# Low bits by PoolE, sign by VectorE, a bias table one block later, and extra matmuls between the first chunks

## The chip, the cores and the metric

One core of a Trainium2 chip runs the kernel. The time is that of one execution on the device in microseconds (us); lower is better. PE is TensorE, DVE is VectorE, ACT is ScalarE, POOL is PoolE (GpSimd), and SP is the engine that issues most DMA transfers. [...]

## What is computed

Three layers follow each other on 4 x 768 = 3072 tokens of width 256. The first is a scan in chunks (8 heads of width 32, state 16), the second a dense two-matrix layer, the third a gated mixture of 8 experts, of which each token takes one.

```python
M = CB * L                                  # within a chunk, L = exp of sums of log a, lower triangle
y = M @ x + (C @ state) * exp(cum)          # plus what the state carries in
state = exp(sum) * state + sum(B x decay)   # from chunk to chunk
h = x @ w_in;  g = max(0.01 * h, h);  x = g @ w_out
logits = x @ w_gate + modality_bias[modality_id];  e = argmax(logits)
out = gate * (max(x @ w1[e], 0) @ w2[e])
```

The weights w_in and w_out come as 64-bit floats. The matrices of the second layer are multiplied as pairs of a rounded high part and a rest, three products for each.

## The kernel before

The scan works in 24 chunks of 128 tokens. The first four (block 0) run ahead of everything else; the other chunks are woven into the matmuls of the dense layer, which runs in six blocks of 512 tokens with 16 steps each (mm1 gives h, mm2 gives y). The expert layer follows at the end.

For each of the first four chunks the loop at L916 calls, in this order: attn_cd (scales C, tile cd), attn_tr (transposes of C and B into ps; from them cbd on VectorE and btt on ScalarE), attn_exp_pe (broadcast matmuls bc, exponentials e on ScalarE, masks of e by affine_select on PoolE), attn_tr2, attn_cb twice (product cb; VectorE multiplies e by it), and p3 (products psy, state st). For chunk 0 the broadcast is built from laT and tri; for chunks 1 to 3 from cumb, a tile with three bfloat16 parts of the running sums. cumb is made by decay: p_212 and p__232 are transposed sums, cr and cumb their residuals on VectorE, cend their last columns, pd a small product of cend.

Between the chunks stand pieces of work from the list early: the loads and splits of w_in and w_out. A piece is 128 x 512 numbers; there are 16. to_f32 (L529) turns the 64-bit words into float32: ScalarE makes hb from the upper half word, PoolE writes lb as whole 32-bit words, VectorE overwrites one 16-bit half of each lb, and then VectorE joins hb and lb. split casts the result to the high part (wih, woh) on ScalarE and subtracts it on PoolE or VectorE into the rest (wil, wol). Loads go to three buffers raw, and each waits until the pieces in its buffer are done.

bias_table makes a table of 3072 x 8 biases from modality_id with six VectorE instructions; block 0's route, in block 1, is the first to read it. The table Q holds the step at which such work is put into the blocks ('bt': 4 is step 4 of block 0).

Nine matmuls of zeros (wps<-zer, bfloat16, 128 x 512) stand at the start. The order on each engine is made by a scheduler from the order in the code; functions named in Q['pin'] keep program order on the engines given there ('t' is PE). Each engine runs its queue in order.

Of the kernel before, what the change touches and what calls it, by code (L numbers as in the profile page):

```python
# [14 lines left out]
ALU = mybir.AluOpType  # L15
# [5 lines left out]
LOW, LOW0 = 0.9 * 2.0 ** -13, 0.2995  # L21
# [3 lines left out]
Q = {'sg': (0, 1),  # L25
 'i00': 0,
 'i01': 1,
 'lo1': -1,
 'o00': 0,
 'o01': 4,  # L30
 'i10': 3,
 'i11': 3,
 'xe': 2,
# [12 lines left out]
 'r0': 6,  # L46
 'r1': 6,
 'xt': 14,
 'bt': 4,
 'cv': 2,  # L50
 'cvn': 3,
 'tr': 4,
# [31 lines left out]
         'L_rows_out': 's',  # L84
         'L_m2_xT': 'v',
         'S_attn_cb': 't',
         'S_split_win': 'g',
         'S_split_wout': 'v',
         'S_load_wout': 'vsg',
# [9 lines left out]
def kernel(  # L99
# [20 lines left out]
    NE, _, F2 = w1.shape  # L120
    P = 128
# [48 lines left out]
    v, s, g, t_ = Pinned(nc.vector, "v"), Pinned(nc.scalar, "s"), Pinned(nc.gpsimd, "g"), Pinned(nc.tensor, "t")  # L170

    def run(fn, args, late=""):
        for e in (v, s, g, t_):
            e.on = e.key in Q["pin"].get(late + fn.__name__, "")
        fn(*args)
        for e in (v, s, g, t_):
            e.on = False
# [351 lines left out]
    def to_f32(raw, q):  # L529

        w = raw.bitcast(I32).rearrange("p (f w) -> p f w", w=2)
        hb = ap_.tile([P, 512], F32, tag="hb", name="hb")
        lb = ap_.tile([P, 512], I32, tag="lb", name="lb")
        s.activation(out=hb, in_=w[:, :, 1].bitcast(F32), func=AF.Copy, scale=2.0 ** -112)
        w4 = raw.bitcast(U16).rearrange("p (f w) -> p f w", w=4)
        l2 = lb.bitcast(U16).rearrange("p (f w) -> p f w", w=2)
        g.tensor_scalar(out=lb, in0=w4[:, :, 3], scalar1=32768.0, scalar2=-(2.0 ** 31), op0=ALU.is_ge, op1=ALU.mult)
        v.tensor_scalar(out=l2[:, :, 0], in0=w4[:, :, 1], scalar1=LOW, scalar2=LOW0, op0=ALU.mult, op1=ALU.add)
        hi = hb.bitcast(I32)
        v.scalar_tensor_tensor(out=hi, in0=hi, scalar=3, in1=lb, op0=ALU.logical_shift_left, op1=ALU.bitwise_or)  # L540
        return hb
# [13 lines left out]
    def split_win(k, kk):  # L555
        r = raws["i", k]
        os = slice(k * 512, (k + 1) * 512)
        f = to_f32(r[:, kk, :], kk) if W64 else r[:, kk, :]
        split(f, wih[:, kk, os], wil[:, kk, os], g if kk in Q["sg"] else v)
# [6 lines left out]
    def split_wout(k, q):  # L566
        r = raws["o", k]
        os = slice(k * 4 + 2 * q, k * 4 + 2 * q + 2)
        f = r[:, 2 * q:2 * q + 2, :].rearrange("p a d -> p (a d)")
        f = to_f32(f, q) if W64 else f  # L570
        split(
            f, woh[:, os, :].rearrange("p a d -> p (a d)"), wol[:, os, :].rearrange("p a d -> p (a d)"), g if q in Q["sg"] else v
        )
# [314 lines left out]
    wt = zer  # L888
    v.memset(wt, 0.0)
    wps = psh.tile([P, 512], F32, tag="h", name="wps")  # L890
    for _ in range(Q["warm"]):
        t_.matmul(wps, lhsT=wt[:, 0:P], rhs=wt, start=True, stop=True)
    nb = len(blocks)
    NC0 = blocks[0][1] // P
    new_xt(0)
# [19 lines left out]
            run(fn, args, "S_")  # L915
    for c in range(NC0):  # L916
        for fn, *args in (
            (attn_cd, c), (attn_tr, c), (attn_exp_pe, c), (attn_tr2, c), (attn_cb, c, 0), (attn_cb, c, 1), (p3, c),
        ):
            run(fn, args, "S_")  # L920
        for fn, args, w in early:
            if w == c:
                run(fn, args, "S_")
# [143 lines left out]
```

## Time and profile before

| | us |
|---|---|
| median of 3 runs | 552.48 |
| lowest, highest | 550.47, 555.38 |
| profiled execution | 552.29 |
| its span | 550.6 |

| engine | busy us | share of the span |
|---|---|---|
| PE | 519.3 | 94% |
| DVE | 365.0 | 66% |
| ACT | 334.0 | 61% |
| POOL | 199.2 | 36% |

The busy shares are means over stages with different limits. The time of the stages and the waits are read from the windows and the time lines below. A busy PE at half clock does half the work.

### The profile page before, as it was taken

The page shows a single profiled execution, that of the slowest core. Times are in us where ns is not written, and L with a number is a line of the kernel's source. Part 1 is how long each engine was busy: PE and PEld are TensorE (multiplying, and loading weights), DVE is VectorE, ACT ScalarE, POOL GpSimd, SP SyncE. Part 2 cuts the span into 40 slices and gives each one's busy share as a digit, 9 for nine tenths or more (in the row PEclk, how much of TensorE's full clock was granted, in tenths as well). Part 3 has the DMA queues.
Part 4 walks back from the last instruction along what each step waited for, and adds up shares of the span by engine and source line. Part 5 has one row for each costly group of instructions (what it writes and reads, how often), then busy time and mean ns, then how long its engine had stood idle before and what let it go on. Part 6 is the DMA issues. An engine that isn't in the chain of part 4 may idle for free.

```text
span 550.6 us, 9529 instructions
## 1 busy us (share of the span) xinstructions
PE 519.3 (94%) x3411; PEld 422.3 (77%) x3411; DVE 365.0 (66%) x714; ACT 334.0 (61%) x699; POOL 199.2 (36%) x167
## 2 busy tenths in 40 slices
PE   6998978999999999999999999999989999999990
PEld 3434654678787878778877787688879999999990
DVE  5658998977667777775667866475577564555630
ACT  5447667675676676765766665354537665666630
POOL 5648798300301120113010301540063466556331
PEclk9559999999999999999999999999999999999996
DMA  8898753212744239322620476345059667777300
GB/s 195 138 226 160 206 143 57 54 34 34 17 116 81 59 43 107 63 59 11 130 60 0 13 139 198 98 31 86 1 187 168 222 210 239 219 236 240 109 23 21
DMA packets 128312, 61.02 MB, mean 111 GB/s; under 512 B 84545, under 2 KB 120514, under 8 KB 128258
## 3 DMA queue, kind: packets, MB, share of 16 engines
q1 hardware_dynamic: 125186, 53.94, 48.2%
q0 software_dynamic: 3072, 6.41, 3.6%
q8 instruction: 29, 0.48, 0.4%
q14 instruction: 25, 0.20, 0.2%
HBM read 53.73 MB, written 6.60 MB: 110 GB/s over the span
## 4 chain that ended last, share of the span: by engine, by line
PE 78%; DVE 8%; issue 5%; ACT 3%; DMA 2%; SPq 1%; POOL 1%; POOLq 0%; DVEq 0%; ACTq 0%
PE y L163 21%; PE h L163 21%; PE hp L163 11%; PE o L163 10%; PE psy L163 5%; PE cb L163 3%; DVE hb L163 1%; DVE gg L163 1%; DMA ct<-in_C_dram 1%; DMA raw<-in_moe_w_in_dram 1%; DVE gl L163 1%; DVE lb L163 1%; PE yr L163 1%; PE pc L163 1%; PE pb L163 1%
## 5 line engine op out<-in xcount | busy, mean ns | idle before, releaser
L163 ACT CAST gh<-gg 128x512 fp32r<-128x512 f32 x96 | 59.6, 621 | 75.6 <-DVE gg L163 74.3
L163 DVE TENSOR_TENSOR gl<-gg,gh 128x512 fp32r<-128x512 f32 x96 | 74.0, 771 | 40.6 <-ACT gh L163 40.0
L163 PE MATMUL h<-xh,wih 128*128 128x512 f32 x192 | 77.7, 408 | 3.9 <-DVE gg L163 3.9
L163 PE MATMUL y<-gl,woh 128*128 128x512 f32 x192 | 76.6, 400 | 3.6 <-DVE gl L163 3.6
L163 DVE TENSOR_TENSOR gg<-sa,h 128x512 f32<-128x512 f32 x96 | 65.3, 681 | 20.5 <-ACT sa L163 20.2
L163 POOL TENSOR_SCALAR_AFFINE_SELECT e<-e 128x1024 f32<-128x1024 f32 (+1 forms) x28 | 28.2, 1012 | 137.9 <-DMA e<-cumd 87.1
L163 PE MATMUL h<-xl,wih 128*128 128x512 f32 x192 | 75.2, 392 | 0.0
L163 PE MATMUL y<-gh,wol 128*128 128x512 f32 x192 | 75.0, 392 | 0.0
L163 PE MATMUL h<-xh,wil 128*128 128x512 f32 x192 | 75.0, 392 | 0.0
L163 PE MATMUL hp<-x2h,w1s 128*128 128x256 f32 x384 | 71.9, 283 | 0.0
L163 PE MATMUL o<-w2s,hh 128*128 128x256 f32 x384 | 69.3, 285 | 0.0
L163 ACT ACTIVATE sa<-h 128x512 f32<-128x512 f32 x96 | 57.2, 596 | 19.0 <-PE h L163 18.4
L163 DVE SCALAR_TENSOR_TENSOR hl<-hp,hh 128x512 fp32r<-128x512 f32 x48 | 33.0, 691 | 52.6 <-ACT hh L163 44.0
L163 PE MATMUL y<-gh,woh 128*128 128x512 f32 x192 | 63.3, 398 | 0.0
L163 PEld LDWEIGHTS hp<-x2h,w1s 128*128 128x128 f32 x384 | 61.1, 192 | 0.6
L163 POOL TENSOR_TENSOR w2s<-r,w2s 128x1024 fp32r<-128x1024 f32 x12 | 34.0, 2838 | 72.7 <-ACT w2s L163 48.7
L163 PEld LDWEIGHTS o<-w2s,hh 128*128 128x128 f32 x384 | 58.4, 191 | 0.4 <-issue 0.4
L163 PE MATMUL hp<-x2l,w1s 128*128 128x256 f32 x192 | 53.3, 283 | 0.0
L163 ACT ACTIVATE hh<-hp 128x512 fp32r<-128x512 f32 x48 | 28.4, 597 | 40.0 <-PE hp L163 35.0
L163 ACT ACTIVATE e<-e,ncum 128x128 f32<-128x128 f32 x160 | 51.5, 395 | 0.0
L163 PE MATMUL o<-w2s,hl 128*128 128x256 f32 x192 | 51.1, 283 | 0.0
L163 POOL DMA_INDIRECT il<-ids,pi x24 | 25.7, 1070 | 66.5 <-DVE pi L163 38.3
(205 smaller groups left out, 1012.3 us busy)
## 6 DMA issues: line engine op xcount, KB each, us to landing
r<-in_moe_w_dram SPq DMA_DIRECT2D x48, 512.0 KB
e<-cumd SPq DMA_DIRECT2D x20, 512.0 KB
raw<-in_moe_w_in_dram SPq DMA_DIRECT2D x4, 1024.0 KB
raw<-in_moe_w_out_dram SPq DMA_DIRECT2D x4, 1024.0 KB
yx<-ysb SPq DMA_DIRECT2D x6, 528.0 KB
xt<-in_x_dram SPq DMA_DIRECT2D x24, 128.0 KB
ct<-in_C_dram SPq DMA_DIRECT2D x24, 64.0 KB
bt<-in_B_dram SPq DMA_DIRECT2D x24, 64.0 KB
```

The lines of the kernel that those rows point to most:

```text
L163: r = f(*args, **kw)
```

## The change

Three edits. In to_f32 PoolE now writes the low bits (multiply and add on half word 1) as whole words of lb, and VectorE the sign (compare and multiply on half word 3) into the upper half of each; before, PoolE wrote the sign and VectorE the low bits into the lower half. bias_table moves from step 4 to step 16, the first step of block 1. And keep puts matmuls of zeros between the parts of each of the first four chunks: 12 or 4, then 2, then 3, in all 44; they are pinned on PE.

```diff
- 'bt': 4,
+ 'bt': 16,
+         'S_keep': 't',
-        g.tensor_scalar(out=lb, in0=w4[:, :, 3], scalar1=32768.0, scalar2=-(2.0 ** 31), op0=ALU.is_ge, op1=ALU.mult)
-        v.tensor_scalar(out=l2[:, :, 0], in0=w4[:, :, 1], scalar1=LOW, scalar2=LOW0, op0=ALU.mult, op1=ALU.add)
+        g.tensor_scalar(out=lb, in0=w4[:, :, 1], scalar1=LOW, scalar2=LOW0, op0=ALU.mult, op1=ALU.add)
+        v.tensor_scalar(out=l2[:, :, 1], in0=w4[:, :, 3], scalar1=32768.0, scalar2=32768.0, op0=ALU.is_ge, op1=ALU.mult)
-    for _ in range(Q["warm"]):
-        t_.matmul(wps, lhsT=wt[:, 0:P], rhs=wt, start=True, stop=True)
+    def keep(n):
+        for _ in range(n):
+            t_.matmul(wps, lhsT=wt[:, 0:P], rhs=wt, start=True, stop=True)
+    keep(Q["warm"])
-            (attn_cd, c), (attn_tr, c), (attn_exp_pe, c), (attn_tr2, c), (attn_cb, c, 0), (attn_cb, c, 1), (p3, c),
+            (attn_cd, c), (attn_tr, c), (attn_exp_pe, c), (keep, 4 if c else 12), (attn_tr2, c), (attn_cb, c, 0), (keep, 2), (attn_cb, c, 1), (keep, 3), (p3, c),
```

The scheduler orders the queues anew. On VectorE, the rows behind the first chunk's cbd stood like this before (the first cbd here is chunk 1's, e is chunk 0's, lb and hb are the first weight piece's):

```order
L163 TENSOR_TENSOR cbd<-ps,gm 128x512
L163 TENSOR_TENSOR cr<-p_212,cumb 64x512
L163 TENSOR_TENSOR bs<-bt,e 128x128
L163 COPY cend<-p__232 32x2
L163 TENSOR_TENSOR cumb<-cr,cumb 32x512
L163 TENSOR_TENSOR cd<-ct,ecum 128x128
L163 COPY cend<-p_212 32x4
L163 TENSOR_TENSOR e<-e,cb 128x512
L163 TENSOR_SCALAR lb<-raw 128x512
```

And now, in the same place (the first lb is that of w_in, the second that of w_out):

```order
L164 TENSOR_TENSOR bs<-bt,e 128x128
L164 TENSOR_SCALAR lb<-raw 128x512
L164 TENSOR_TENSOR cr<-p_212,cumb 64x512
L164 COPY cend<-p__232 32x2
L164 SCALAR_TENSOR_TENSOR hb<-hb,lb 128x512
L164 TENSOR_TENSOR cd<-ct,ecum 128x128
L164 TENSOR_SCALAR lb<-raw 128x512
L164 TENSOR_TENSOR cbd<-ps,gm 128x512
L164 TENSOR_TENSOR cumb<-cr,cumb 32x512
L164 COPY cend<-p_212 32x4
L164 TENSOR_TENSOR e<-e,cb 128x512
```

Two weight pieces moved ahead of cumb, and chunk 1's cbd behind both.

On PoolE, from chunk 2's masks on, the rows stood like this before (128x512 are masks of the first four chunks, two for each; 128x1024 are masks of later chunks, whose e is loaded):

```order
L163 AFFINE_SELECT e<-e 128x512 x2
L163 TENSOR_TENSOR wil<-hb,wih 128x512
L163 AFFINE_SELECT e<-e 128x512 x2
L163 TENSOR_SCALAR lb<-raw 128x512
L163 AFFINE_SELECT e<-e 128x1024 x3
L163 TENSOR_TENSOR wil<-hb,wih 128x512
L163 TENSOR_SCALAR lb<-raw 128x512 x2
L163 AFFINE_SELECT e<-e 128x1024
```

And now:

```order
L164 AFFINE_SELECT e<-e 128x512 x2
L164 AFFINE_SELECT e<-e 128x1024 x3
L164 AFFINE_SELECT e<-e 128x512
L164 AFFINE_SELECT e<-e 128x1024
L164 AFFINE_SELECT e<-e 128x512
L164 TENSOR_SCALAR lb<-raw 128x512
L164 TENSOR_TENSOR wil<-hb,wih 128x512
L164 TENSOR_SCALAR lb<-raw 128x512 x3
```

Chunk 3's two masks moved behind masks of later chunks, and the fourth piece's lb behind all of them.

On PE, from chunk 1's first broadcast matmuls on (each dummy is a LDWEIGHTS and a MATMUL; there are seven at the first "..."), the rows now are:

```order
L164 MATMUL bc<-negm,cumb 128x512
...
L164 MATMUL pd<-cend,bsel 128x6 x4
L164 MATMUL cb<-cbd,btt 128x512
L164 LDWEIGHTS zer
L164 MATMUL wps<-zer 128x512
...
L164 MATMUL ps<-ident,bt 128x128
L164 MATMUL psy<-e,xt 32x128 x8
L164 MATMUL psy<-xt,bs 64x128 x2
```

Chunk 0's second cb and its psy stand behind chunk 1's bc and pd, as before; new are nine dummies between that cb and psy.

## Rows read from the trace of the kernel before

**Rows 1.** Windows: busy us (instructions) of each engine, granted clock, DMA share, GB/s.

```profile
14.00:15.00 1.00, 1.00 (x3) 0.13 (x2) 0.48 (x1) 0.75 (x3) 0.59 (x1) 0.83 0.86 104
15.00:38.00 23.00, 22.79 (x100) 10.73 (x100) 12.86 (x27) 9.87 (x22) 11.67 (x11) 0.50 0.89 176
34.00:38.00 4.00, 4.00 (x16) 2.09 (x17) 2.25 (x5) 2.27 (x5) 0.86 (x2) 0.50 1.10 328
38.00:39.00 1.00, 1.00 (x5) 0.07 (x1) 0.59 (x2) 0.27 (x1) 1.00 (x2) 0.72 1.25 274
39.00:105.00 66.00, 57.67 (x313) 36.62 (x313) 60.14 (x94) 44.15 (x104) 53.78 (x33) 1.00 0.56 128
105.00:500.00 395.00, 390.92 (x2629) 332.41 (x2626) 265.50 (x543) 251.22 (x522) 105.61 (x84) 1.00 0.51 103
```

**Rows 2.** Time line of PE: start us, us, instruction, count, idle before and releaser.

```profile
1.27 3.65 PE L163 MATMUL wps<-zer 128*128 128x512 bf16 x9 [1.27 <-DVE zer L163]
...
12.84 0.33 PE L163 MATMUL ps<-ident,cd 128*128 128x128 f32 x1 [2.25 <-ACT btt L163]
...
14.66 0.61 PE L163 MATMUL bc<-negm,cumb 96*128 96x512 bf16 x1
...
16.49 0.45 PE L163 MATMUL ps<-ident,ct 128*128 128x128 f32 x1
...
17.25 1.87 PE L163 MATMUL pd<-cend,bsel 32*128 32x6 f32 x8
19.05 2.08 PE L163 MATMUL cb<-cbd,btt 64*128 64x512 f32 x4
...
40.76 1.13 PE L163 MATMUL cb<-cbd,btt 64*128 64x512 f32 x4
...
43.12 0.67 PE L163 MATMUL psy<-cdt,st 128*128 128x256 f32 x2 [0.86 <-DVE st L163]
43.72 0.64 PE L163 MATMUL psy<-e,xt 128*32 128x128 f32 x16
44.30 0.44 PE L163 MATMUL psy<-xt,bs 128*64 128x128 f32 x4
```

**Rows 3.** Tiles lb, hb and e: ns min/median/max, first and last start, forms.

```profile
L163 POOL TENSOR_SCALAR lb<-raw x16: 1953/2038/2467, 12.6 to 94.5; 128x512 int32<-128x512 uint16 x16
L163 DVE TENSOR_SCALAR lb<-raw x16: 439/508/1549, 17.5 to 97.2; 128x512 uint16<-128x512 uint16 x16
L163 DVE SCALAR_TENSOR_TENSOR hb<-hb,lb x16: 673/688/1750, 19.8 to 100.1; 128x512 int32<-128x512 int32 x16
L163 POOL TENSOR_TENSOR wil<-hb,wih x8: 1267/1296/1699, 22.6 to 96.9; 128x512 fp32r<-128x512 f32 x8
L163 POOL TENSOR_SCALAR_AFFINE_SELECT e<-e x16: 629/866/1547, 11.0 to 109.3; 128x512 f32<-128x512 f32 x8, 128x1024 f32<-128x1024 f32 x8
```

**Rows 4.** Groups of DVE, 38 to 106 us: count, busy us, mean ns, idle before.

```profile
L163 DVE CAST m<-modi 128x24 f32<-128x24 int32 x1 | 1.1, 1065 | 0.0
L163 DVE TENSOR_SCALAR m<-m 128x24 f32<-128x24 f32 x2 | 0.8, 382 | 0.0
L163 DVE TENSOR_TENSOR btab<-btab,bt 128x192 f32<-128x192 f32 x1 | 0.4, 357 | 0.0
```

**Rows 5.** Time line of DVE: cumb, and the fourth piece's lb.

```profile
13.80 0.68 DVE L163 TENSOR_TENSOR cumb<-cr,cumb 32x512 bf16<-32x512 f32 x1 [0.31 <-ACT cumb L163]
...
41.56 1.18 DVE L163 TENSOR_SCALAR lb<-raw 128x512 uint16<-128x512 uint16 x1
```

**Rows 6.** Time line of POOL: lb of the first, second and seventh piece.

```profile
12.63 1.96 POOL L163 TENSOR_SCALAR lb<-raw 128x512 int32<-128x512 uint16 x1
16.09 2.29 POOL L163 TENSOR_SCALAR lb<-raw 128x512 int32<-128x512 uint16 x1 [1.49 <-DMA raw<-in_moe_w_out_dram]
...
51.66 1.98 POOL L163 TENSOR_SCALAR lb<-raw 128x512 int32<-128x512 uint16 x1 [0.69 <-POOL e L163]
```

**Rows 7.** Chain of waits in block 1: start us, us, what.

```profile
107.20 1.36 PE h L163 x6
```

## The prediction

> **What bounds the kernel now.** I read the windows by stage first, then the time lines of the engines in the first 55 us, then the tiles of the weight split. The windows [rows 1] cut the run by TensorE's granted clock and by who is full. [...] From 39 to 105 us it is full, VectorE is busy 60.1 of 66 us, PoolE 53.8, and PE still has 8.3 us idle. From 105 to 500 us PE is busy 390.9 of 395 us. So after 105 us PE is the bound, and nothing in the diff touches that work: whatever the change does is a shift of the two stages before, and the shift goes one for one into the end.
>
> The first stage is the four chunks of the scan. PE waits 2.25 us before 12.84 us, the clock falls two microseconds later, and it comes back only after 34 to 38 us, where PE is busy 4.00 of 4 us, the last of it with 512-column products; with the narrow matmuls before, PE was busy too and the clock stayed low [rows 1, 2]. The fourth chunk's last matmul ends at 44.30 + 0.44 = 44.74 us [rows 2].
>
> The second stage splits the weights in 16 pieces: for each a PoolE lb (1.95 us at best), a VectorE lb and hb, a cast on ScalarE, and a PoolE subtraction (1.27) [rows 3]. VectorE is nearly full there, in part with waiting: the same lb takes 0.44 at best and 1.55 at worst, hb 0.67 and 1.75 [rows 3].
>
> **The change, part by part.**
>
> *Bias table.* Of its six VectorE instructions at about 74.6 to 78.2 us the cast takes 1.1 us, two scalings together 0.8, an addition 0.4; two products like the addition make it 2.9 us at most, and since neighbouring rows overlap a little I take 2.5 [rows 4]. They leave a stretch where VectorE is full and go to block 1, where VectorE is idle 129.5 of 395 us and the full PE hides them [rows 1]. Without that cover, where one of them delays a gl that PE waits for, the same 2.5 us come back. Gain 2.5 us, bounds 0 and 2.9.
>
> *Low bits and sign swapped.* Each piece keeps one PoolE instruction of 128x512 from 16-bit words into 32-bit words and one VectorE instruction from 16-bit to 16-bit; only the operations in them change places. On VectorE I take the same 0.44 us, bounds 0.44 and the 0.67 of hb. On PoolE no row shows a multiply and add. The lowest row of this size is the affine_select at 0.63 us, the two-input subtraction takes 1.27, the row that it replaces 1.95 to 2.47 [rows 3]. I take 1.95, the row with the same source, destination and number of operations, and keep 0.63 and 2.47 for the range.
>
> *Its place in the queues.* Here I expect the gain of the dummies to go. In the new VectorE order two lb stand ahead of cumb, the residual that chunk 1's broadcast matmuls bc load. Before, cumb ran at 13.80 us and bc began at 14.66 [rows 2, 5]. Now cumb is behind the second lb, whose PoolE instruction waits for the first piece of w_out: that landed at 16.09 us [rows 6]. The loads issued up to it stand in the same order as before, so it lands no earlier. Then PoolE 1.96 to 2.29 us, to 18.05 or 18.4; lb 0.44; cbd of chunk 1 and cumb, 0.6 and 0.6: bc of chunk 1 begins at about 20.0 us, 5.3 us late. Queued behind it on PE are pd, the cb products, nine dummies and the first chunk's psy.
>
> *The dummies.* They are 44 (12 + 3x4 + 4x2 + 4x3). Fourteen stand ahead of that bc and fill time in which PE would wait anyway: no cost. But PE then waits for the late cend (to about 15.9 us) and for cumb (to 20.0), some 5 us of the last 7, more than the gap after which the clock fell before. So I take half clock at 20.0 us. From there at half: bc 1.8 us (14.66 to 16.49), pd 1.8 (17.25 to 19.05), cb 1.0 (two in 2.08), seven dummies at 0.41 (nine in 3.65 at the start, near twice the 0.227 of the full clock) 2.9: 7.5 us, to 27.5 us [rows 2]. This stretch ends as dense with 512 columns as the one after which the clock came back, so I let it come back there. The rest of the four chunks at full clock: 23 dummies at 0.227 (six matmuls in 1.36 us) [rows 7] 5.2; six cb at 0.53 (two in 1.13) 3.2; four psy at 1.0 (43.72 to 44.74) 4.0; three state products at 0.6 (43.12 to 43.72) 1.8; two bc at half of 1.8, 1.8; nine transposes at 0.19 (two in 0.76 at half clock) 1.7 [rows 2]. That is 17.7 us, and the fourth chunk ends at 45.2 us against 44.74: **+0.5 us**.
>
> *PoolE's order.* Chunk 3's masks now stand among four masks of later chunks that wait for their broadcast loads, and the fourth split's lb behind them. Before, that split's VectorE lb ran at 41.56 us [rows 5]. Now PoolE is free for it at about 43.4 (chunk 3's product must be masked 1.8 us ahead of 45.2), lb to 45.4; VectorE's lb, cbd and hb to 47.1, the cast to 47.7, the subtraction to 49.0, three more lb to 55.0 us. Before, the same seventh lb ended at 51.66 + 1.98 = 53.6 [rows 6]. **+1.4 us** on the split chain, bounds 0 (VectorE's idle takes it up) and 3.
>
> *Sum.* +0.5 + 1.4 - 2.5 = -0.6 us. The profiled execution took 552.29 us (span 550.6 and 1.7 around it), 0.2 under the median of 552.48. So about **551.5 us**.
>
> **The rivals.**
>
> R1, multiply and add is cheaper on PoolE. At the 1.27 us of the subtraction, bc of chunk 1 comes 0.7 us earlier and the 13 pieces after 39 us leave PoolE 9 us. Of that the end sees no more than the 8.3 us that PE is idle there [rows 1]; PoolE's wait is one of several, so I put half, 4 us in all: 547.5 us. At 0.63 us, the whole of it: 544. For it speaks that 1.95 us is long beside 1.27 for two inputs; against it, that the kinds of words, the length and the number of operations stay. [...] The affine_select, a compare too, takes 0.63 us here and speaks against a dear compare.
>
> R2, the dummies hold the clock: it does not fall, or is back by 20 us. Then the 7.5 us are 1.6 + 0.9 + 0.9 + 0.5 = 3.9, the fourth chunk ends at 41.6 us, and the lag of the split chain goes: -0.6 - 3.6 - 1.4, about 546.7 us. For it: 14 dummies stand where before PE did little. Against it: the two waits that the late cend and cumb make.
>
> R3, the other side: the dummies run at half clock and so only cost. If it does not rise at 27.5 us, 23 dummies take 9.4 us and the other 12.5 us double: the fourth chunk ends at 61.9 us, +17 us, 568 us. Each microsecond of half clock past 27.5 costs half of one, so it passes 1% if the clock is still low at about 40 us. For it: before, PE was busy for 23 us at half clock without release. Against it: that work was narrow, and four dense microseconds ended it [rows 1].
>
> **How the numbers follow.** About 1%, 5.5 us, is what a measurement of this kernel can tell from no change. Forecast 0.50 (its own range 548 to 556), R1 0.23, R2 0.12, R3 0.15 (half of it late by a few us only, 554 to 558, half above). Faster by over 1% (under 547): nearly half of R1, over half of R2, a little of the forecast, 0.21. Slower (over 558): half of R3 and a little of the forecast, 0.12. Within: 0.67. A range from 545 to 557.5 leaves out a quarter of R1 and of R2 below, half of R3 above, and little of the forecast.
>
> **What would show it.** Right: a granted clock of 0.5 around 20 us and 1.0 before 30; VectorE's second lb just after 18 us and bc of chunk 1 at about 20; chunk 3's psy ending near 45; no bias rows near 75 and VectorE still full there; PoolE's lb at 1.95. Wrong: PoolE's lb at 1.3 or less; a clock that never falls; bc at 15; half clock past 30 us.

## The result and the profile after

| | before | changed |
|---|---|---|
| median, us | 553.51 | 561.65 |
| lowest to highest | 550.47 to 555.38 | 560.95 to 562.76 |
| profiled execution | 552.29 | 561.41 |
| its span | 550.6 | 559.7 |

The ratio is 1.0147, 95% interval 1.0117 to 1.0178: the changed kernel is slower by 1.5%, where 551.5 us (545 to 557.5) was forecast. Three experiments below, e7, e9 and e13, have executions 8 to 12 us apart, some of which the ratios leave out, so nothing is built on one of them alone.

The engines' busy times of the changed kernel: PE 526.6 us, VectorE 361.4, ScalarE 331.9, PoolE 177.9 (199.2 before). First the windows of the changed kernel by TensorE's granted clock, which is 1.00 at its full level and never under 0.50 in the windows of any run here (columns as in [rows 1]):

```profile
16.00:26.00 10.00, 9.28 (x30) 4.55 (x30) 5.69 (x12) 5.53 (x14) 4.75 (x6) 0.50 0.98 162
...
27.00:50.00 23.00, 20.34 (x151) 9.03 (x150) 11.62 (x25) 6.04 (x17) 8.56 (x10) 1.00 0.93 181
50.00:53.00 3.00, 3.00 (x8) 1.05 (x7) 2.63 (x5) 2.75 (x10) 2.35 (x3) 0.53 0.28 46
53.00:105.00 52.00, 44.49 (x217) 28.64 (x217) 44.46 (x68) 36.38 (x86) 27.92 (x26) 0.99 0.49 128
```

The lower clock now lasts from 16 to 26 us, where it lasted from 15 to 38 [rows 1]. That part of the change works. What it bought is gone by 50 us: PE idles 2.7 us between 27 and 50, the clock is low once more from 50 to 53, and PE idles 7.5 us from 53 to 105. The time line of PE over the four chunks:

```profile
15.08 1.16 PE L164 MATMUL cb<-cbd,btt 64*128 64x512 f32 x2 [1.73 <-DVE cend L164]
...
18.19 0.63 PE L164 MATMUL bc<-negm,cumb 96*128 96x512 bf16 x1
...
21.83 2.07 PE L164 MATMUL cb<-cbd,btt 64*128 64x512 f32 x2
23.84 2.87 PE L164 MATMUL wps<-zer 128*128 128x512 bf16 x7
26.64 1.12 PE L164 MATMUL cb<-cbd,btt 64*128 64x512 f32 x2
...
41.62 1.12 PE L164 MATMUL cb<-cbd,btt 64*128 64x512 f32 x2
42.68 0.60 PE L164 MATMUL wps<-zer 128*128 128x512 bf16 x2
43.22 1.12 PE L164 MATMUL cb<-cbd,btt 64*128 64x512 f32 x2
...
47.76 0.43 PE L164 MATMUL psy<-e,xt 128*32 128x128 f32 x8 [2.01 <-DVE e L164]
48.35 0.42 PE L164 MATMUL psy<-e,xt 128*32 128x128 f32 x8 [0.17 <-DVE e L164]
48.71 0.44 PE L164 MATMUL psy<-xt,bs 128*64 128x128 f32 x4
49.62 0.78 PE L164 MATMUL h<-xh,wih 128*128 128x512 f32 x2 [0.47 <-ACT xh L164]
```

The fourth chunk ends at 48.71 + 0.44 = 49.15 us, 4.4 us behind the 44.74 of before [rows 2], and the last thing it waits for is e. The chain of waits leads from there to PoolE and to a transfer:

```profile
37.85 6.82 DMA e<-cumd
...
44.81 1.69 POOL e L164 x2
...
46.92 1.30 DVE e L164 x2
...
48.35 0.82 PE psy L164 x12
```

And the time line of PoolE (128x512 are masks of the first four chunks; a row x2 with 128x1024 holds one of a later chunk and one of chunk 3):

```profile
32.60 1.22 POOL L164 TENSOR_SCALAR_AFFINE_SELECT e<-e 128x512 f32<-128x512 f32 x2 [4.67 <-ACT e L164]
36.93 1.23 POOL L164 TENSOR_SCALAR_AFFINE_SELECT e<-e 128x1024 f32<-128x1024 f32 x1 [3.11 <-DMA e<-cumd]
39.80 1.09 POOL L164 TENSOR_SCALAR_AFFINE_SELECT e<-e 128x1024 f32<-128x1024 f32 x1 [1.64 <-DMA e<-cumd]
42.00 1.68 POOL L164 TENSOR_SCALAR_AFFINE_SELECT e<-e 128x1024 f32<-128x1024 f32 x2 [1.10 <-DMA e<-cumd]
44.81 1.68 POOL L164 TENSOR_SCALAR_AFFINE_SELECT e<-e 128x1024 f32<-128x1024 f32 x2 [1.14 <-DMA e<-cumd]
46.58 0.74 POOL L164 TENSOR_SCALAR lb<-raw 128x512 int32<-128x512 uint16 x1
```

Each mask of a later chunk waits for its broadcast load, and chunk 3's two masks, which wait for nothing of that kind, stand behind the third and the fourth: ScalarE has done their e by 40.52 + 1.09 = 41.61 us, and PoolE still stands idle for 1.14 us before 44.81. The fourth piece's lb runs at 46.58; before, VectorE's part of that piece had run at 41.56 already [rows 5]. The tiles of lb are the surprise (minimum/median/maximum ns, against [rows 3]):

```profile
L164 POOL TENSOR_SCALAR lb<-raw x16: 641/666/969, 13.2 to 95.2; 128x512 int32<-128x512 uint16 x16
L164 DVE TENSOR_SCALAR lb<-raw x16: 447/458/1348, 13.9 to 100.2; 128x512 uint16<-128x512 uint16 x16
```

PoolE's instruction is three times cheaper, 0.67 us for 2.04, and yet nothing is gained. Where this went is in the waits from 45 to 105 us (engine, tile, what for: us in all, times, longest), of the changed kernel and then of the kernel before:

```profile
POOL lb L164 <- DVE hb L164: 11.8, 7, 5.1
...
DVE gl L164 <- ACT gh L164: 6.3, 4, 3.2
```

```profile
POOL lb L163 <- DVE hb L163: 3.7, 4, 1.6
...
DVE gl L163 <- ACT gh L163: 1.7, 3, 0.7
```

PoolE now waits 11.8 us for VectorE's hb (3.7 before), and VectorE 6.3 us for ScalarE's gh (1.7 before).

**A ledger of PE.** To set kernels side by side, the span of each is cut into windows of 1 us. PE's idle time is what is not busy in them; the half-clock loss is the busy time times (1 - granted clock), what the same work would have saved at the full clock, by the measure of cb near enough (one alone took 2.07 us at 0.50 and 1.12 at 1.00; 21.83 and 26.64 us above); the rest of the span is work. Each row is one profiled execution. The sums over the span, in us:

| kernel | span | idle | half-clock loss | work |
|---|---|---|---|---|
| before | 550.6 | 31.3 | 11.8 | 507.5 |
| changed | 559.7 | 33.1 | 6.5 | 520.2 |
| difference | +9.1 | +1.8 | -5.4 | +12.7 |

In this form the result is short: the engine that bounds the kernel has 12.7 us more work, the clock gives back 5.4, and PE waits no less than before.

### The profile page after: what moved, and what is told of

The parts are those of the page before. It is cut to its first block, busy times and chain, and to the rows that moved or that the text cites. A ratio compares the mean times of both kernels' runs of the same rounds, so it can differ in the third digit from the quotient of the medians.

```text
span 559.7 us, 9611 instructions
## 1 busy us (share of the span) xinstructions
PE 526.6 (94%) x3455; PEld 424.6 (76%) x3455; DVE 361.4 (65%) x714; ACT 331.9 (59%) x699; POOL 177.9 (32%) x167
## 4 chain that ended last, share of the span: by engine, by line
PE 74%; issue 7%; DVE 6%; DMA 5%; ACT 3%; POOL 2%; SPq 1%; POOLq 0%; DVEq 0%; ACTq 0%
PE h L164 22%; PE y L164 22%; PE hp L164 8%; PE o L164 8%; PE psy L164 5%; PE cb L164 3%; DMA out_dram<-o,gi 2%; DVE hb L164 2%; DMA e<-cumd 1%; DMA raw<-in_moe_w_out_dram 1%; PE wps L164 1%; DVE lb L164 1%; POOL out_dram L164 1%; PE pc L164 1%; PE pb L164 1%
## 5 line engine op out<-in xcount | busy, mean ns | idle before, releaser
L164 DVE TENSOR_TENSOR gl<-gg,gh 128x512 fp32r<-128x512 f32 x96 | 72.2, 753 | 48.3 <-ACT gh L164 45.2
L164 POOL TENSOR_TENSOR w2s<-r,w2s 128x1024 fp32r<-128x1024 f32 x12 | 33.3, 2771 | 68.0 <-ACT w2s L164 52.7
L164 PEld LDWEIGHTS h<-xh,wih 128*128 128x128 f32 x192 | 36.3, 189 | 18.2 <-DVE gg L164 9.4
L164 ACT ACTIVATE hh<-hp 128x512 fp32r<-128x512 f32 x48 | 28.0, 598 | 36.8 <-PE hp L164 33.3
```

The lines of the kernel that those rows point to most:

```text
L164: r = f(*args, **kw)
```

## The experiments

Theory M says that the dummies' new order lost the time: they put chunk 3's masks behind the broadcast loads. Theory D says that the dummies' own time on PE lost it. The rivals are the two other edits.

**One edit at a time.** e1 has the dummies alone, e2 the swap alone, e3 the bias table alone, e4 the swap and the bias table.

```diff
 e1:  + (keep, 4 if c else 12), ... (keep, 2), ... (keep, 3)        + 'S_keep': 't'
 e2:  + g.tensor_scalar(out=lb, in0=w4[:, :, 1], ..., op0=ALU.mult, op1=ALU.add)
      + v.tensor_scalar(out=l2[:, :, 1], in0=w4[:, :, 3], ..., op0=ALU.is_ge, op1=ALU.mult)
 e3:  - 'bt': 4,   + 'bt': 16,
 e4:  e2 and e3
```

> Only the 44 dummies are added to the kernel before. Theory (the dummies move the masks): the new order on PoolE, in which chunk 3's two masks stand behind masks of later chunks that wait for their broadcast loads, comes with the dummies alone, so chunk 3's psy ends at 47 to 50 us here too (49.15 in the changed kernel, 44.74 before) and the time is 3 to 7 us above the kernel before: 556.5 to 560.5 us. Rival (the swap costs: two lb ahead of cumb hold up chunk 1): without the swap bc of chunk 1 begins near 14.7 us, the clock is back earlier than 26 us, chunk 3 ends before 44.7 us and the time is 548 to 554 us.

> Only the swap of low bits and sign in the weight split is made. Theory (the dummies cost, the swap helps): PoolE's lb takes 0.65 us instead of 2.0, PoolE is no longer busy 53.8 of the 66 us from 39 to 105, and part of the 8.3 us that PE is idle there goes: 547 to 552 us. Rival (the swap costs): with a lb ahead of cumb on VectorE chunk 1 begins late, chunk 3 ends 2 us or more behind 44.7 and the time is 556 us or more. A third possibility: PoolE's time was no limit there at all, 553 to 555 us, with VectorE's hb as the one that all wait for.

> Only the bias table is moved from block 0 to block 1. By the term of the sum (2.5 us of VectorE work leaves a stretch in which VectorE is full): 550 to 552 us, 1 to 3 below the kernel before. Rival (VectorE's full stretch is full with waiting, so the 2.5 us only become idle time): 553 to 554 us, no change. If the new order that the scheduler makes costs by itself: 556 us or more.

> The swap and the bias table, without the dummies. Theory (the dummies' order costs what was lost): 546 to 552 us, faster than the kernel before, with chunk 3's masks on PoolE ahead of those of later chunks and its psy ending by 45 us. Rival (the swap or the bias table costs): 557 us or more, like the changed kernel at 561.7.

| | median us | ratio to before | interval |
|---|---|---|---|
| e1, dummies | 561.26 | 1.0169 | 1.0117 to 1.0221 |
| e2, swap | 554.77 | 1.0056 | 1.0032 to 1.0080 |
| e3, bias table | 552.16 | 0.9996 | 0.9962 to 1.0031 |
| e4, swap and bias table | 554.05 | 1.0028 | 0.9996 to 1.0060 |

The dummies alone cost all that the change costs. The time line of PE in e1 has the same wait, longer:

```profile
46.70 0.43 PE L164 MATMUL psy<-e,xt 128*32 128x128 f32 x8 [4.12 <-DVE e L164]
```

and the time line of PoolE in e1 the same reason, at the first of the later chunks' masks:

```profile
37.43 1.09 POOL L164 TENSOR_SCALAR_AFFINE_SELECT e<-e 128x1024 f32<-128x1024 f32 x1 [6.97 <-DMA e<-cumd]
```

In e1's profile the clock stays full up to 20 us and is low in the four chunks only from 20 to 24. The windows of e1:

```profile
8.00:20.00 12.00, 11.77 (x81) 7.32 (x81) 7.34 (x17) 8.52 (x23) 6.82 (x6) 1.00 0.96 192
20.00:24.00 4.00, 4.00 (x11) 1.61 (x11) 1.98 (x4) 0.62 (x1) 4.00 (x4) 0.58 1.12 194
```

PE hardly waits in the 12 us ahead of that fall. e11 below has the same dummies and no swap either, and its clock is low from 16 to 26 us, so the two lb ahead of cumb are not what sets the place of the fall. In e1 the chain reaches chunk 3's products earlier, and so waits longer for the same loads.

The swap alone is a little slower, not faster. The windows from 65 to 80 us, of the kernel before and then of e2:

```profile
65.00:80.00 15.00, 11.91 (x59) 8.30 (x58) 14.83 (x24) 9.99 (x22) 14.36 (x9) 1.00 0.66 190
```

```profile
65.00:80.00 15.00, 10.88 (x44) 6.82 (x43) 14.93 (x23) 8.79 (x21) 8.56 (x8) 0.85 0.67 190
```

PoolE is busy 8.6 of 15 us where it had been busy 14.4, VectorE 14.9 as before (14.8). PE's idle time from 45 to 125 us falls by 0.8 us in the ledger (7.2 to 6.4), but its clock drops twice there, for a loss of 3.3 us that the kernel before doesn't have. The waits of e2 from 45 to 105 us tell where PoolE's saving went:

```profile
POOL lb L163 <- DVE hb L163: 12.8, 7, 3.4
...
DVE gl L163 <- ACT gh L163: 4.1, 6, 1.2
```

The bias table moved for nothing: its six instructions no longer stand near 75 us, and the time is the same within 0.35%.

**The orders mended.** e5 is the changed kernel with the masks of later chunks queued behind chunk 3's on PoolE. e6 has VectorE's lb queued behind cumb too. e11 is e1 with the masks mended, and e8 is e4 with lb behind cumb.

```diff
 attn_exp_pe:  + ch["mask"] = g.affine_select(...)
 attn_mask:    + with tc.issue_after(ch["mask"].ins):     # order only, no wait
 decay:        + ch["cumb"] = v.tensor_tensor(out=cumb[32:64], ...)      (e6, e8)
 to_f32:       + with tc.issue_after(ch["cumb"].ins):                    (e6, e8, around VectorE's lb)
```

> The changed kernel, with one thing undone: on PoolE the masks of later chunks are queued behind chunk 3's masks, as in the kernel before. Theory M (the wait of chunk 3's masks behind broadcast loads is what was lost): PE no longer waits near 46 us, the fourth piece's lb runs near 40 instead of 46.6 us, chunk 3's psy ends at 45 to 46 us instead of 49.2, and the time is 4 us below the changed kernel's 561.7: 556.5 to 558.5 us. Theory D (the dummies' own time on PE is what was lost: 44 at 0.227 us are 10 us, of which the clock gives back 5): PE comes earlier to the dense layer and then waits longer for the weight split; 560 to 562 us.

> The changed kernel with chunk 3's masks ahead of the later ones, and with VectorE's lb queued behind cumb too. Theory M with the second part: bc of chunk 1 begins near 15 us instead of 18.2, the clock holds to about 24 us as with the dummies alone, chunk 3 ends at 42 to 44 us, and the time is 2 to 3 us below that with the masks alone: 553.5 to 556 us. Theory D: PE's ten microseconds of dummies stay and the weight split sets the end of block 0; 558 us or more.

> The swap and the bias table, no dummies, with VectorE's lb queued behind cumb. If a lb ahead of cumb is what eats the swap's gain: 550 to 552 us, 2 to 4 us below the same kernel without that order (554.05). If PoolE's time was no limit in the split stage (VectorE's hb and the raw loads are): 553 to 555 us, no change.

> The 44 dummies alone, with chunk 3's masks ahead of later ones on PoolE. Theory (order): the 4.1 us that PE waited at 46.7 us with the dummies alone goes, chunk 3 ends near 43 us instead of 48.6, and the time is 553 to 556 us instead of 561.3. By the ledger (work +12, half-clock loss -10, idle -1) it lands within 2 us of the kernel before. If it stays above 558 us, the masks' order isn't the cause.

| | median us | ratio to before | interval |
|---|---|---|---|
| e5, masks first | 554.60 | 1.0057 | 1.0024 to 1.0090 |
| e6, masks and cumb first | 552.90 | 1.0045 | 1.0022 to 1.0067 |
| e8, e4 with cumb first | 554.93 | 1.0085 | 1.0044 to 1.0127 |
| e11, dummies, masks first | 553.38 | 1.0027 | 0.9993 to 1.0062 |

One order on PoolE is worth 1.0147 - 1.0057 = 0.9%, 5 us, in the changed kernel, and 1.0169 - 1.0027 = 1.4%, 8 us, with the dummies alone. In e5 the masks run where ScalarE's e releases them:

```profile
41.45 1.22 POOL L164 TENSOR_SCALAR_AFFINE_SELECT e<-e 128x512 f32<-128x512 f32 x2 [7.37 <-ACT e L164]
```

and PE goes through chunk 3 without a wait:

```profile
45.40 0.60 PE L164 MATMUL psy<-cdt,st 128*128 128x256 f32 x2
45.93 0.64 PE L164 MATMUL psy<-e,xt 128*32 128x128 f32 x16
46.51 0.44 PE L164 MATMUL psy<-xt,bs 128*64 128x128 f32 x4
```

It ends at 46.95 us instead of 49.15. These 2.2 us are part of the 5; the same order also brings the fourth piece's lb on PoolE from 46.58 to 42.75 us, and no run parts the two. Theory M holds for the larger part. What it leaves is a kernel that is still not faster, and there theory D takes over; the ledger, with all kernels that have 44 dummies:

| kernel | span | idle | half-clock loss | work |
|---|---|---|---|---|
| before | 550.6 | 31.3 | 11.8 | 507.5 |
| e1, 44 | 558.2 | 30.2 | 6.7 | 521.2 |
| e5, 44 | 554.3 | 28.1 | 6.8 | 519.4 |
| e6, 44 | 552.9 | 28.3 | 5.1 | 519.5 |
| e11, 44 | 553.7 | 27.4 | 6.3 | 520.0 |
| e2, e3, e4, e8: none | 550.8 to 553.4 | 28.5 to 33.3 | 12.3 to 16.8 | 507.2 to 509.4 |

With the 44 dummies PE has 12 to 14 us more work. Summed by tile in the same way, the dummies themselves are 10.4 to 10.7 us of it, 0.24 each (in the changed kernel's chunk 3 nine of them stand in 0.95 + 0.54 + 0.66 = 2.15 us). Most of the rest is cb: 1.2 us more in the changed kernel, 2.3 in e1. One cb of a chunk takes its operands from partitions 0 to 63, the other from 64 to 127 (hs in attn_cb), and the two of a pair ran side by side, 1.13 us for both at the full clock. Each leaves two records, one after the other, 32 for the 16 cb of this form in either kernel, so a row x4 is a pair and a row x2 is one alone. The tile cb in the half microsecond from 40.7 us in the kernel before and from 41.6 in the changed one (x2 are the first records of a pair, which start together), and one alone in the kernel before:

```profile
L163 PE MATMUL cb<-cbd,btt x2: 693/693/693, 40.8 to 40.8; 64*128 64x512 f32 x2
```

```profile
L164 PE MATMUL cb<-cbd,btt x1: 693/693/693, 41.6 to 41.6; 64*128 64x512 f32 x1
```

```profile
23.21 2.07 PE L163 MATMUL cb<-cbd,btt 64*128 64x512 f32 x2
```

A pair takes as long as one cb: 2.08 us at half clock (19.05 in [rows 2]) for 2.07, and 1.13 at the full clock (40.76, a later chunk's) for 1.12. The dummies stand between the two cb of each chunk, and the four chunks have no pair left, where they had two before (19.05 and 37.23 us). Over the whole kernel four pairs become three in the changed kernel and two in e1 and e11, at 1.06 us each. No run has the dummies elsewhere, with the pairs left whole.

With both orders mended, e6 gets back 6.7 us of half clock and 3.0 of idle time: 12.0 - 6.7 - 3.0 = +2.3, its span against that of before. So at their best the 44 do not quite pay for themselves. e8 gave no gain from cumb alone, against the first of its two expectations.

**Fewer dummies, or better placed.** e7 is e6 with the 17 of chunk 0 only. e9 is e11 with those of chunks 0 and 1 (26). e10 is e6 with 26 and eight more behind chunk 0's first cb. e13 is e9 with those eight, and e14 has 12, 8 and 3 in chunk 0 only.

```diff
 e7:   (keep, (12, 0, 0, 0)[c]) ... (keep, ( 2, 0, 0, 0)[c]) ... (keep, (3, 0, 0, 0)[c])
 e9:   (keep, (12, 4, 0, 0)[c]) ... (keep, ( 2, 2, 0, 0)[c]) ... (keep, (3, 3, 0, 0)[c])
 e10:  (keep, (12, 4, 0, 0)[c]) ... (keep, (10, 2, 0, 0)[c]) ... (keep, (3, 3, 0, 0)[c])
 e13:  as e10, without the swap and with 'bt': 4
 e14:  (keep, (12, 0, 0, 0)[c]) ... (keep, ( 8, 0, 0, 0)[c]) ... (keep, (3, 0, 0, 0)[c]), as e13
```

> As the kernel with both orders mended, with dummies only in chunk 0: 17 instead of 44, so 27 x 0.227 = 6.1 us less of them. Theory D (each dummy behind the clock's rise costs its 0.227 us): if the clock still holds, 4 to 6 us below that kernel, 548 to 551 us. If the later dummies are what holds the clock, it stays at half into 35 us and the gain is gone: 553 to 556 us. Theory M (dummies cost nothing, only their order did): within 1 us of that kernel.

> The kernel before with dummies in the first two chunks only (12 or 4, 2, 3: 26 in all) and with chunk 3's masks ahead of later ones on PoolE; no swap, bias table where it was. By the ledger (span = PE's idle time + half-clock loss + work): 26 dummies add 6 to 7 us of work, and if the clock holds behind chunk 1 as in the kernel with all 44, the half-clock loss goes from 11.8 to about 2 us; chunk 3 ends near 40 us and the time is 547 to 550 us, 2 to 4 below the kernel before. Rival (the dummies of chunks 2 and 3 hold the clock): it falls again by 35 us, loss 8 us or more, 554 us or above.

> The changed kernel with both orders mended, dummies in the first two chunks only, and eight more of them behind chunk 0's first cb, where PE waited 1.46 us (34 in all). If that wait is what lets the clock fall near 19 us: it holds to 20 us or later, half-clock loss below 3.4 us, and with 10 dummies fewer than 44 (2.3 us) the time is 548 to 551 us, below the 552.9 of the same kernel with 44. Rival: the clock falls as before and the loss stays at 3.4 or more; 551 to 554 us.

> The kernel before with chunk 3's masks first on PoolE and 34 dummies: those of the first two chunks and eight more behind chunk 0's first cb. If the fill holds the clock: no execution near 560 us, half-clock loss below 2 us in the profile, work 10 us above the kernel before, so 548 to 552 us, from 3 us faster to no change. If the number of dummies is too dear: 552 to 556 us. If the clock still falls in some executions: a spread of 549 to 560 us as with 26.

> The same with 23 dummies, all in chunk 0 (12, 8, 3). If the fill alone holds the clock: work only 7 us above the kernel before, loss below 3 us, 546 to 550 us. If the dummies of chunk 1 are needed: the clock falls by 25 us, and the time is 551 to 560 us.

| | median us | ratio | interval | loss | work |
|---|---|---|---|---|---|
| e7, 17 | 559.28 | 1.0061 | 1.0000 to 1.0122 | 16.3 | 512.9 |
| e9, 26 | 557.42 | 1.0140 | 1.0054 to 1.0227 | 3.3 | 515.5 |
| e10, 34, swap | 554.66 | 1.0082 | 1.0047 to 1.0117 | 1.6 | 518.0 |
| e13, 34 | 560.33 | 1.0096 | 1.0054 to 1.0138 | 8.0 | 516.8 |
| e14, 23 | 556.18 | 1.0064 | 1.0029 to 1.0099 | 9.0 | 516.4 |

None beats the kernel before. Loss and work are those of one execution. e7's took 560.04 us, where others of it go down to 550.09; e9's took 549.13 us, its others up to 560.56, at mean granted clocks from 0.986 down to 0.963, so its median counts and not its best. e10 bears on the question of the clock. In e6 PE has one long wait, and the clock falls behind it; time line and windows of e6:

```profile
16.34 0.33 PE L164 MATMUL ps<-ident,cd 128*128 128x128 f32 x1 [1.46 <-ACT btt L164]
```

```profile
18.00:19.00 1.00, 1.00 (x8) 0.98 (x8) 1.00 (x2) 0.84 (x2) 0.99 (x1) 0.73 0.64 197
19.00:25.00 6.00, 6.00 (x12) 2.10 (x13) 4.12 (x6) 1.59 (x4) 4.50 (x5) 0.50 0.88 168
```

In e10, with eight more matmuls in that wait, it holds up to 46 us. The windows of e10:

```profile
18.00:46.00 28.00, 21.93 (x155) 9.80 (x155) 16.31 (x34) 13.55 (x37) 13.75 (x15) 1.00 0.94 196
46.00:50.00 4.00, 3.73 (x10) 1.65 (x11) 3.78 (x9) 2.71 (x10) 2.92 (x4) 0.57 0.77 89
```

So the clock can be held through all four chunks, which end at 40.8 us here, four earlier than before, and it brings nothing: PE idles 6.1 of those 28 us. In e13 and e14, with the same fill, it holds up to 33 and 40 us. That the wait by itself lets the clock fall is not shown: in e1 it fell with hardly a wait ahead of it. The time line of PE shows the longest of these waits, and that of VectorE whose it is:

```profile
46.27 1.22 PE L164 MATMUL h<-xh,wih 128*128 128x512 f32 x2 [4.06 <-ACT xh L164]
```

```profile
44.40 0.29 DVE L164 TENSOR_TENSOR cd<-ct,ecum 128x128 f32<-128x128 f32 x1 [4.12 <-DMA ct<-in_C_dram]
```

VectorE stands at a later chunk's cd, which waits for the load of its ct, and hb, which ScalarE's wih ahead of xh waits for, is queued behind it. It is so in e13 too (4.10 us at 45.49, PE's h waits 3.29 us, the clock low from 47 to 53, after a first fall from 33 to 37) and in e14, where st is behind that cd. PE in e14:

```profile
42.70 1.19 PE L164 MATMUL psy<-cdt,st 128*128 128x256 f32 x2 [5.45 <-DVE st L164]
```

The loads of the next chunks, all issued on SP, are what comes next once PE is early; PE then waits in one piece, and by the end of that wait the clock that was held is down to the lower level: 0.53 in the microsecond from 46 in e10, 0.50 from 47 in e13 and from 41 in e14.

**The price on PoolE.** e12 keeps the kernel before but for one instruction: PoolE multiplies and adds on the half word that it compared before.

```diff
- g.tensor_scalar(out=lb, in0=w4[:, :, 3], scalar1=32768.0, scalar2=-(2.0 ** 31), op0=ALU.is_ge, op1=ALU.mult)
+ g.tensor_scalar(out=lb, in0=w4[:, :, 3], scalar1=0.0, scalar2=0.0, op0=ALU.mult, op1=ALU.add)
```

> The kernel before, with PoolE's compare and multiply on half word 3 replaced by a multiply by 0 and an add of 0 on the same half word (the sign is left out of the weights); VectorE's instruction stays as before. If the operation sets PoolE's price: lb at 0.65 us on PoolE, as with the swap. If the half word that is read sets it: 1.95 us. The time is 553 to 556 us by the run with the swap alone, where PoolE's cheaper lb brought nothing.

```profile
L163 POOL TENSOR_SCALAR lb<-raw x16: 637/663/969, 12.4 to 88.8; 128x512 int32<-128x512 uint16 x16
```

With the same half word read, 0.66 us for 2.04: the two operations set the price here; which of the two does is not told apart. The whole took 578.58 us: the weights have lost their sign, and the last stage has more matmuls (hp<-x2h 416 for 384); the stages ahead of it can still be compared. The last of block 0, VectorE's first copy yt<-y, starts at 116.25 us against 116.03 before (118.28 in e2): PoolE's 16 x 1.37 us less change nothing there either.

## Why the prediction was wrong, point by point

**The bound** was right for the most part: 7.3 of the 9.1 us that the span is longer are there when y's copy of block 0 starts (116.03 us before, 123.36 now). The other 1.8 came later, against "one for one", and are not explained.

**The clock** was about right. Half clock was put at 20.0 to 27.5 us and lay at 16 to 26; R2 (the clock is held) did not come, and of R3 (half clock past 30 us) only the 3 us from 50 to 53. It was held for longer where eight matmuls filled a wait (to 46, 33 and 40 us in e10, e13 and e14). The prediction's reading that before 34 us only narrow matmuls ran at half clock doesn't hold: the cb at 23.21, above, has 512 columns, as have those at 28.87 and 32.70. Why the clock came back at 38 us in the kernel before is not shown.

**The place in the queues** was right in kind and late by 1.8 us: cumb did stand behind two lb and the landing of w_out, but bc began at 18.19 and not at 20.0, since PoolE's lb took 0.66 us.

**The dummies' term, +0.5 us, is the step that failed first.** It priced a cb at 0.53 us, "two in 1.13", and at half clock at 1.0. Both rows of [rows 2] are read rightly, but they are pairs that run side by side. The change puts dummies between the two cb of a chunk, so their price is that of one alone; before, too, only four of the eight cb had a partner. In the changed kernel each cb of the four chunks stands alone, and it takes 42.68 - 41.62 = 1.06 us, at half clock 23.84 - 21.83 = 2.01. Six cb at 1.06 are 3.2 us more than was summed, the one at half clock 1.0 more. With the 2.2 us of waits below and 1.8 us that bc was earlier, that is 3.2 + 1.0 + 2.2 - 1.8 = 4.6, close to the 3.9 us between the forecast end of chunk 3 (45.2) and the measured (49.15). With no pairs the sum would have said +4.7 instead of +0.5 for this term alone, and 555.7 in all.

**PoolE's order** was seen, and mis-sized. The step let chunk 3's masks come in time and priced only the lag of the fourth lb, +1.4 us. It should have asked when the four broadcast loads land: at 36.9, 39.8, 42.0 and 44.8 us by the rows of PoolE above, the last 1.4 us behind the 43.4 at which PoolE was put free of them. PE waits 2.2 us for it, and undoing that order gives back 5 us (e5).

**The swap** was taken at 1.95 us on PoolE, with 0.63 as the bound. The bound was the truth, R1's condition came true, and its price did not: no microsecond of it came to the end (e2, e12). PoolE was busy 53.8 of 66 us there [rows 1], but VectorE's hb and, behind it, ScalarE's gh end the waits that PE sees; 16 cheaper instructions turn into PoolE's 12.8 us of waiting for hb (e2). Why the two pairs of operations are 1.3 us apart on PoolE (1.95 and 0.64 at best) is not shown.

**The bias table** gave 0 of the 2.5 us (e3, to within 2 us). The six instructions take less than they seemed, too. The group of the cast in the changed kernel, from 105 to 150 us:

```profile
L164 DVE CAST m<-modi 128x24 f32<-128x24 int32 x1 | 0.2, 172 | 0.0
```

172 ns, and 1065 at 74.6 us [rows 4]. A price read from one stretch need not be the price that the instruction has in another. And "VectorE is nearly full, in part with waiting" was in the prediction's own text: time taken from such a stretch turned into other waits.

**The sum** put a gain in a stage that gives none (-2.5) beside two costs that were too small (+0.5 and +1.4); all three errors had the same sign. With +4.7, 5 us for PoolE's order and 0 for the bias table, less the 1.8 us that bc was earlier, it would have come to 560.0 us, against 561.65; it is put together afterwards, and what lies between is open.

**What stays open.** What makes the clock fall, why the executions of e7, e9 and e13 lie so far apart, and whether dummies that leave the cb pairs whole would pay. The swap's small loss (0.6%, e2) goes with 3.3 us of half clock from 68 to 84 us, which e12, as cheap on PoolE, does not have; that this is its cause was read from single profiles and not tried apart.

## What to carry to other kernels

Dummy matmuls are work on the engine that bounds the kernel: multiply their number by their price first (0.24 us each here), set against it the half-clock loss that the profile shows (busy time times one minus the clock), and put them only where PE waits anyway, not between two matmuls that would run side by side (1.06 us for each pair parted here). When a change reorders a queue, ask of each moved instruction which transfer now stands ahead of it and when that lands. And before you take a price from a row, look what ran beside it, and whether the change leaves it there: the cast took 1065 ns in one place and 172 in the other.

## What the runs showed of the hardware

On PoolE, from 16-bit words into 32-bit words of 128 x 512, compare and multiply takes 1.95 to 2.04 us, multiply and add on the same half word 0.64 to 0.66. Two float32 matmuls of 64 rows and 512 columns, one with its operands in partitions 0 to 63 and one in 64 to 127, took 1.13 us together and one alone 1.12 (2.08 and 2.07 at half clock). A wait of PE of 1.46 us was followed by a fall of the clock some 2 us after its end (e6), and the same stretch with matmuls of zeros in the wait kept it for 28 us (e10); in e1 it fell with PE busy 11.77 of the 12 us ahead. VectorE's small cast took 1065 ns while PoolE's 1.55 us mask ran beside it and 172 ns while PoolE stood still, each measured once; whether the mask is the cause was not tried.
